# Seven half-width block products in place of eight for the output projection (Strassen's scheme), with a new plan of the instruction order

## The chip, the cores and the metric

The kernel runs on one core of one Trainium2 chip. The metric is device microseconds of an execution. Times are medians of several executions on the chip; the profile is of one execution, whose "span" runs from its first to its last instruction and is 1.7 to 1.8 us shorter than the time. "Rounds" run two or more kernels in turn, so that their times can be compared.

## The reference, cut to what matters

Attention for 4 x 8 heads of 768 tokens, of which three heads see all earlier keys and five see 4 sink keys and a window of 64; then a gated feed-forward block with its own residual gate on the 3072 x 512 result.

```python
g = x @ w_gate                       # 3072x512 @ 512x1536
gelu = 0.5 * g * (1.0 + erf(g * inv_sqrt2))
val = x @ w_val
ffn_out = gelu * val @ w_out         # 3072x1536 @ 1536x512: the product that changes
res_gate = 1.0 / (1.0 + np.exp(-(x @ w_res)))
return x + res_gate * ffn_out
```

## The kernel before

The program is a graph of tasks; a planner puts them into one order per engine with the help of priorities, and waits are derived from the dependences. The tokens are worked on in six chunks of four row tiles of 128. Attention of a chunk is laid between the gate/value stages and the output product of the chunk before it. `hT` holds the hidden values, transposed, 12 blocks of 128; `wo` is the output weight. One row tile of the output costs 12 matmuls of 512 columns:

```python
    def output(c, h, htoks, xbuf, xtoks, xtbuf, xttoks):
        for lt in range(4):
            ...                                        # residual product, 4 matmuls of 512, then tanh on ScalarE
            fb = Buf(P_ps, "gv" if last else "out")    # one PSUM bank
            for j in range(6):
                prev_t = G.add("pe", ..., e.matmul(at(fb)[:, w], lhsT=at(h)[:, fi, s], rhs=wo[:, fi, w],
                                                   start=(fi == 0), stop=(fi == NF - 1))   # fi = 2j, 2j+1; line 1161
            t1 = G.add("dve", ..., scalar_tensor_tensor(out=ot, in0=sr, scalar=1.0, in1=fb, op0=add, op1=mult))
            t2 = G.add("dve", ..., tensor_tensor(out=ot, in0=ot, in1=xbuf, op=add))
            G.add("sp", ..., dma_start(out[...], ot))
```

At the start GpSimd issues all loads into one queue (q, k, v, then gate and value weights `wg`, `wv` in pieces of 512 KB) and builds the masks in between. TensorE runs padding matmuls on a blank tile between the first attention pieces while it has to wait for data. `va` are the loaded values, `vs` their copies shifted by half a tile.

The softmax here doesn't subtract the row's maximum and nothing guards it: scores larger than these inputs give would overflow.

Of the kernel before, what the change touches and what calls it, by code (L numbers as in the profile page):

```python
# [4 lines left out]
NHEAD = 8  # L5
SEQ = 768
# [33 lines left out]
DT_FIRST = 2  # L40
DT_ALL = 9
# [5 lines left out]
    "0:-96.05 3:-32.5 13:-14.98 398:-205.14 399:-3161.01 400:-242.48 401:-60.67 406:194.11 428:585.68 "  # L47
    "430:523.84 442:461.16 444:1172.07 587:-105.78 592:-108.69 613:396.07 617:407.42 620:-11.7 640:556.2 "
    "642:106.88 643:194.09 646:-2979.21 649:-102.44 659:511.02 686:-2.88 687:77.5 695:496.52 696:499.45 "
    "698:-3129.77 703:60.14 704:-184.95 705:-133.38 707:183.02 708:380.49 711:7.46 712:149.85 713:-50.64 "  # L50
    "715:-14.97 722:1121.95 725:480.98 726:449.69 731:-39.24 732:60.67 733:-318.24 737:-43.72 738:419.39 "
    "739:143.85 743:67.93 744:-230.75 746:-318.2 749:428.99 755:137.07 756:5.66 757:60.69 761:-9.34 "
    "762:495.92 764:2489.99 778:1098.32 789:2479.4 791:2501.2 807:953.41 837:1156.8 842:1419.06 877:2567.99 "
    "879:1563.79 880:2429.98 883:2507.13 898:1013.73 933:1964.55 937:1029.47 939:1471.24 940:2476.14 "
    "955:3421 962:3506.26 963:3575.25 971:3584.03 984:2490.73 989:3565.66 1020:3589.17 1022:2520.47 "
    "1036:2494.69 1066:3486.98 1103:3422.44 1109:3530.5 1114:4315.61 1115:4410.02 1124:-926.78 1134:4596.47 "
    "1141:3465.41 1143:2510.98 1146:2495.35 1152:4653.43 1157:112.2 1170:3039.97 1193:107.93 1248:3488.54 "
    "1265:3479.95 1266:4395.47 1271:4430.01 1272:4484.04 1275:-26.92 1284:5420.01 1289:3472.11 1290:4444.38 "
    "1293:-34.14 1295:3453.61 1302:4490.78 1305:3510.02 1316:3998.02 1318:3550.85 1319:3550.87 1320:4107.35 "
    "1349:3529.55 1351:5429.99 1355:3583.42 1414:5485.04 1451:1066.16 1462:4552.31 1474:4473.03 1475:6343.89 "  # L60
    "1480:4497.31 1530:6505.9 1534:2349.36 1556:5501.98 1602:6498.99 1637:6513.87 1670:7448.62 1687:7406.44 "
    "1689:5504.27 "
# [399 lines left out]
def build_kernel(nc, q, k, v, w_gate, w_val, w_out, w_res, out):  # L462
# [15 lines left out]
    P_st = Pool(many("qks", 2, [128, 4096], FP16))  # L478
# [5 lines left out]
    P_er = Pool(many("er", 2, [128, 4608], FP16))  # L484
# [5 lines left out]
    P_h = Pool(many("hT", 2, [128, NF, 512], FP16))  # L490
# [7 lines left out]
        "av1": (2, one(0, 1)), "av2": (1, [(0, 1)]), "av1": (3, one(0, 1, 6)),  # L498
        "sc": (2, [(2, 3), (4, 5)]), "scr": (3, one(5, 4, 3, 2)), "scr0": (3, one(5, 4, 3, 2)),
# [3 lines left out]
    def at(buf):  # L503
        if buf.pool is P_ps:
            return psum[:, buf.slot[0] * 512:(buf.slot[-1] + 1) * 512]
        return buf.pool.items[buf.slot]
# [50 lines left out]
    wtok = {}  # L557
# [20 lines left out]
    late_copies = []  # L578

# [10 lines left out]
    def values(b, a, z, base, each, on_engines=False):  # L590

        BB = batch(b)
        for i in range(a, z):
            BB.vtok[i] = dma("pool", base, 0.9, (lambda i=i: lambda: at(BB.v)[:, i, :, 0:DHEAD])(),
                             v[b, :, i * 128:(i + 1) * 128, :].rearrange("h p d -> p h d"), bufs=[BB.v])
            BB.vtok[i].late = 1.3
# [37 lines left out]
        for lo in cuts:  # L634
            hi = lo + 1 if each else z
            ts = []
            for dst, src, off in ((0, 64, 1), (64, 0, 0)):
# [3 lines left out]
                    [BB.vtok[i - off] for i in range(lo, hi)], base + 1, bufs=[BB.v, BB.vs], dma=0.15 * (hi - lo),  # L641
                    name="vs", grp=("vs", b, lo)))
# [5 lines left out]
    def loads_rows(c, si, b, a, z):  # L648
# [3 lines left out]
        st = Buf(P_st)  # L652
# [5 lines left out]
        def sv(j, h0, h1, w):  # L658
            return at(st)[:, :].rearrange("p (j h w) -> p j h w", j=2, h=NHEAD)[:, j, h0:h1, 0:w]
        for gi, (h0, h1) in enumerate(groups):  # L660
            for j, src in enumerate((q, k)):
                t = dma("pool", base + 4 * gi + j, (h1 - h0) * n * 0.089,
                        (lambda j=j, h0=h0, h1=h1: lambda: sv(j, h0, h1, n * 64))(),
                        src[b, h0:h1, lo:hi, :].rearrange("h (p j) d -> p h (j d)", j=n), bufs=[st])
# [6 lines left out]
        for k_ in range(0, NPAIR, per):  # L671
            ps_ = ORDER[k_:k_ + per]
            pr = 1000 * c - 492 + ps_[0] if c else 40 * k_ - 205
            for js in (((1,), (0,)) if c == 0 else ((0, 1),)):
# [3 lines left out]
                def tr(e, items=items, scr=scr):  # L678
                    return [e.transpose(out=at16(scr)[64 * x:64 * x + 64, (m * n + i) * 128:(m * n + i + 1) * 128],  # L679
                                        in_=at(st)[:, (jj * NHEAD + h) * 256 + i * 64:(jj * NHEAD + h) * 256 + (i + 1) * 64],  # L680
                                        identity=ident[:, :])
                            for m, (p, jj) in enumerate(items) for i in range(n) for x, h in enumerate(PAIRS[p])]
                tt = G.add("pe", c_mm(128, n) * len(items), tr, [t_ident] + [tok[jj, h] for p, jj in items for h in PAIRS[p]],
                           pr, bufs=[st, scr], name="qkT")
# [18 lines left out]
    def loads_natural(c, si, b, a, z):  # L703
# [3 lines left out]
        st = Buf(P_st)  # L707
# [4 lines left out]
        for i in range(a, z):  # L712
            for j, src in ((1, k), (0, q)):
                def sv(i=i, j=j):
                    return at(st)[:, (j * 4 + i - a) * 512:(j * 4 + i - a + 1) * 512]
# [4 lines left out]
                for d in ds:  # L720
                    d.late = 5.0
                t = G.add("sp", 1.65, (lambda sv=sv, i=i, j=j: lambda e: e.dma_start(
                    at(BB.qkt)[:, j, :, i * 128:(i + 1) * 128], sv(), transpose=True))(), ds, base, bufs=[st, BB.qkt], dma=0.6, name="dT")
                t.late = 3.0
# [7 lines left out]
        t.late = 2.0  # L732
# [8 lines left out]
    def attention(c, segs, xbuf, xtbuf, xtoks, xttoks, l0=0, last=(), ek=None):  # L741
# [6 lines left out]
        for k_, p in enumerate(order):  # L748
# [34 lines left out]
            P.et = Buf(P_er if any(retr) else P_es)  # L783
            P.where, P.ready = {}, {}
            P.off = 0
            for g in range(0, len(banks), 2):
                scores(P, tiles, [t[1:] + (id(t[2]) in lower,) for t in banks[g:g + 2]], g, retr)
            todo.append(P)
# [295 lines left out]
    def gate_value(c, xtbuf, xttoks, halves=()):  # L1084
        h = Buf(P_h)
        toks = []
        ph(c, "table").append(G.add("act", 0.2, lambda e: e.activation(out=scratch[:, :], in_=ident[:, 0:1], func=AF.Gelu),
# [190 lines left out]
```

## Time and profile before

| | kernel before |
|---|---|
| time, median (48 executions, those beside the result and all later runs) | 270.71 us (270.27 to 271.70) |
| span of the profile | 268.8 us |
| TensorE busy, matmuls | 98%, 2391 |
| VectorE busy | 140.1 us (52%) |
| output product, sum of start distances of its matmuls | 64.0 us |
| start of the last padding matmul | 18.52 us |

The sum of start distances is a better measure of TensorE than its "busy" time, because the ends of matmuls are modelled and overlap: the profile gives a matmul of 512 columns 0.38 us, while the next one starts 0.216 us after it.

In the profile's lines PE is TensorE's matmuls, PEld its weight loads, DVE VectorE, ACT ScalarE, POOL GpSimd and SP SyncE.

### The profile page before, as it was taken

The numbers are of one execution on the slowest core, as the hardware profiler recorded it, in microseconds if no ns is written. First come the engines' busy times: TensorE is split into PE (matmuls) and PEld (weight loads), VectorE is DVE, ScalarE is ACT, GpSimd is POOL, SyncE is SP. The second block draws the span as 40 slices with busy tenths as digits, with TensorE's granted clock in tenths as the row PEclk, the third lists the DMA queues.
The fourth block names the chain that finished last, engine by engine and source line by source line (L and its number), as shares of the span: only waits on it lengthen the run. The fifth ranks groups of instructions, "written<-read, shape, count | busy, mean of one in ns | idle before, by whom it ended". The sixth has DMA issues, their size and how long they took to land.

```text
span 268.8 us, 5676 instructions
## 1 busy us (share of the span) xinstructions
PE 264.2 (98%) x2391; PEld 138.7 (52%) x2391; DVE 140.1 (52%) x273; ACT 139.9 (52%) x215; POOL 87.3 (32%) x124
## 2 busy tenths in 40 slices
PE   8999999999999999999999999999999999999995
PEld 7677465465444455444455444555444455444444
DVE  2698245485264376445476433486145367534344
ACT  3785358783334877136792243984233788233310
POOL 8999508995808029894000000000000000000000
DMA  6999999999999999999994100022000113200013
GB/s 86 171 205 207 185 180 228 169 168 187 171 129 187 154 160 185 216 189 125 184 148 134 41 0 0 2 41 96 25 0 0 39 41 80 78 2 0 1 39 120
DMA packets 97562, 29.38 MB, mean 109 GB/s; under 512 B 85504, under 2 KB 93952, under 8 KB 97536
## 3 DMA queue, kind: packets, MB, share of 16 engines
q0 software_dynamic: 70320, 14.69, 65.5%
q1 hardware_dynamic: 27216, 14.33, 27.9%
q8 instruction: 19, 0.31, 0.5%
q14 instruction: 7, 0.06, 0.1%
HBM read 29.36 MB, written 6.29 MB: 133 GB/s over the span
## 4 chain that ended last, share of the span: by engine, by line
PE 93%; DMA 3%; POOL 1%; DVE 1%; issue 0%; POOLq 0%; DVEq 0%
PE ps L1116 44%; PE ps L1161 23%; PE ps L1146 8%; PE ps L857 5%; PE ps L991 3%; DMA va<-in_v_dram 3%; PE ps L1098 3%; PE ps L981 2%; PE ps L1005 2%; PE ps L1070 1%; POOL qks L555 1%; PE ps L948 1%; PE ps L679 1%; PE ps L1178 1%; DVE otile L1168 0%; DVE otile L1165 0%
## 5 line engine op out<-in xcount | busy, mean ns | idle before, releaser
L1130 DVE SCALAR_TENSOR_TENSOR hT<-gact,ps 128x512 f16<-128x512 f16 x68 | 45.8, 686 | 67.4 <-ACT gact L1128 36.6
L1128 ACT ACTIVATE gact<-ps 128x512 f16<-128x512 f32 x68 | 40.1, 597 | 74.0 <-PE ps L1116 72.5
L1116 PE MATMUL ps<-xT,wv 128*128 128x512 f16 x272 | 74.3, 379 | 0.0
L1116 PE MATMUL ps<-xT,wg 128*128 128x512 f16 x272 | 74.1, 379 | 0.0
L1161 PE MATMUL ps<-wo,hT 128*128 128x512 f16 (+2 forms) x312 | 70.4, 363 | 0.0
L1116 PEld LDWEIGHTS ps<-xT,wg 128*128 128x128 f16 x272 | 26.3, 98 | 31.5 <-ACT xT L1077 0.6
L1116 PEld LDWEIGHTS ps<-xT,wv 128*128 128x128 f16 x272 | 26.2, 98 | 30.5 <-DVE hT L1130 0.5
L1161 PEld LDWEIGHTS ps<-wo,hT 128*128 128x128 f16 x312 | 27.5, 98 | 27.0 <-issue 0.7
L873 ACT ACTIVATE er<-ps 128x1024 f16<-128x1024 f32 (+4 forms) x40 | 34.2, 891 | 9.5 <-PE ps L857 9.4
L555 POOL DMA_DIRECT2D qks<-in_k_dram x36 | 28.3, 827 | 32.4 <-DMA qkt<-qks 21.9
L555 POOL DMA_DIRECT2D qks<-in_q_dram x36 | 28.8, 840 | 0.8 <-POOLq L1260 0.8
L1165 DVE SCALAR_TENSOR_TENSOR otile<-srs,ps 128x512 f32<-128x512 f32 (+2 forms) x26 | 16.8, 644 | 16.5 <-PE ps L1161 16.4
L1146 PE MATMUL ps<-wr,xT 128*128 128x512 f16 x96 | 24.7, 379 | 0.0
L555 POOL DMA_DIRECT2D va<-in_v_dram x24 | 21.6, 926 | 2.7 <-PE ps L1005 2.7
L1149 ACT ACTIVATE srs<-ps 128x512 f32<-128x512 f32 x24 | 14.3, 597 | 15.6 <-PE ps L1146 15.3
L1048 DVE TENSOR_TENSOR xtok<-ps,rcp 128x512 f32<-128x512 f32 (+1 forms) x28 | 16.9, 609 | 0.6
L1168 DVE TENSOR_TENSOR otile<-otile,xtok 128x512 f32<-128x512 f32 (+2 forms) x26 | 16.8, 647 | 0.7
L857 PE MATMUL ps<-qkt 64*128 64x64 f16 (+4 forms) x391 | 16.9, 213 | 0.0
L857 PEld LDWEIGHTS ps<-qkt 64*128 64x128 f16 x391 | 9.8, 94 | 9.4 <-issue 3.4
L873 ACT ACTIVATE es<-ps 128x1024 f16<-128x1024 f32 (+1 forms) x14 | 12.6, 898 | 2.9 <-PE ps L857 2.6
L1146 PEld LDWEIGHTS ps<-wr,xT 128*128 128x128 f16 x96 | 8.7, 98 | 10.0 <-issue 0.7
L1178 PE MATMUL ps<-blank 128*128 128x128 f16 x116 | 11.4, 249 | 1.1 <-DVE blank L527 1.1
(70 smaller groups left out, 212.5 us busy)
## 6 DMA issues: line engine op xcount, KB each, us to landing
out_dram<-otile SPq DMA_DIRECT2D x23, 256.0 KB, 2.2
va<-in_v_dram POOLq DMA_DIRECT2D x24, 128.0 KB, 17.0
qks<-in_k_dram POOLq DMA_DIRECT2D x32, 64.0 KB, 11.9
qks<-in_q_dram POOLq DMA_DIRECT2D x32, 64.0 KB, 12.4
wg<-in_moe_w_gate_dram POOLq DMA_DIRECT2D x3, 512.0 KB, 10.3
wv<-in_moe_w_val_dram POOLq DMA_DIRECT2D x3, 512.0 KB, 10.6
wo<-in_moe_w_out_dram POOLq DMA_DIRECT2D x4, 384.0 KB, 22.2
vs<-va SPq DMA_DIRECT2D x4, 260.0 KB, 7.4
```

The lines of the kernel that those rows point to most:

```text
L555: return G.add(eng, issue, lambda e: e.dma_start(out_ap(), in_ap), deps, prio, bufs=bufs, dma=cost, name=name, grp=grp)
L857: return [e.matmul(at(scr)[:, oo:oo + w], lhsT=side(BB, low, 1)[half, k0:k0 + 128], rhs=side(BB, low, 0)[half, qq:qq + w], start=True, sto ...
L873: return e.activation(out=o, in_=i_, func=AF.Exp, scale=SM_SCALE)
L1048: t2 = G.add("dve", c_dve(2 * n * 64), lambda e: e.tensor_tensor(out=xview(), in0=avv(0, DHEAD), in1=scale(), op=ALU.mult), [t1] + xdeps, ...
L1116: return lambda e: [e.matmul(at(dst)[:, :], lhsT=w[:, ci, f * 128:(f + 1) * 128], rhs=at(xtbuf)[:, ci, :], start=(ci == 0), stop=(ci == NC ...
L1128: ta = G.add("act", c_act(512), (lambda gb=gb, ga=ga: lambda e: e.activation(out=at(ga)[:, :], in_=at(gb)[:, :], func=AF.Gelu))(), [tg], p ...
L1130: th = G.add("dve", c_dve(512), (lambda vb=vb, ga=ga, f=f: lambda e: e.scalar_tensor_tensor(out=at(h)[:, f, :], in0=at(ga)[:, :], scalar=0 ...
L1146: e.matmul(at(rb)[:, :], lhsT=at(xtbuf)[:, ci, s], rhs=wr[:, ci, :], start=(ci == 0), stop=(ci == NCB - 1))
L1149: ta = G.add("act", c_act(512), (lambda rb=rb, sr=sr: lambda e: e.activation(out=at(sr)[:, :], in_=at(rb)[:, :], func=AF.Tanh, scale=0.5)) ...
L1161: e.matmul(at(fb)[:, w], lhsT=at(h)[:, fi, s], rhs=wo[:, fi, w], start=(fi == 0), stop=(fi == NF - 1))
L1165: t1 = G.add("dve", c_dve(n), (lambda fb=fb, sr=sr, ot=ot, w=w: lambda e: e.scalar_tensor_tensor(out=at(ot)[:, w], in0=at(sr)[:, w], scala ...
L1168: t2 = G.add("dve", c_dve(n), (lambda ot=ot, lt=lt, w=w: lambda e: e.tensor_tensor(out=at(ot)[:, w], in0=at(ot)[:, w], in1=at(xbuf)[:, lt, ...
```

## The change

Two row tiles and twelve blocks are taken as a 2 x 2 by 2 x 2 block product, which seven products of half width compute instead of eight. Each is six matmuls of 256 columns. The sums of hidden blocks and the differences of weights that the scheme needs go to VectorE; copies and additions of the partial results go to VectorE and ScalarE. It is used for chunks 1 to 4 and for the first half of chunk 5. `hT` becomes one buffer, staging for q and k becomes three halves in place of two wholes, PSUM pairs are shared more widely, the copy of head 6 stands ahead of the shifted values in SyncE's queue, the tiles of the attention weights (`er`, two of 4608 columns) become one of 4608 and one of 2816, and longer transfers are assumed in the plan. The priorities of the planner are new, so the whole order of instructions changes. The core, with cuts:

```diff
+FAST = (1, 2, 3, 4, 5)
-    P_h = Pool(many("hT", 2, [128, NF, 512], FP16))
+    P_h = Pool(many("hT", 1, [128, NF, 4, 128], FP16))
+    P_hs = Pool(many("hS", 1, [128, 3, NF // 2, 2, 128], FP16))
+    wt = sb("wt", [128, 4, NF // 2, 256], FP16)
...
-        "sc": (2, [(2, 3), (4, 5)]), ...
+        "sc": (3, [(2, 3), (4, 5), (0, 1)]), ...
...
+                    order=copies[-1:], name="vs", grp=("vs", b, lo)))
...
+    def sums(c, h, htoks):                     # VectorE, in the gate/value stage; S3 replaces A21 in hT
+            t1 = add(0, (0, 1), (1, 1), ALU.add, deps, "s1")
+            t2 = add(1, 0, (0, 0), ALU.subtract, [t1], "s2")
+            t4 = add(2, (1, 0), 1, ALU.subtract, [t2], "s4")
+            t3 = add((0, 1), (0, 0), (0, 1), ALU.subtract, [t1], "s3")
...
+    def output_fast(c, pi, h, htoks, hs, stoks, xbuf, xtoks, xtbuf, xttoks):
+        X, Y = Buf(P_ps, "out"), Buf(P_ps, "out")          # two banks, used in turn
+        p1 = product(X, "A11", "B11", True, [])
+        k1 = keep(p1, 0, 0)                                # copy out of X, VectorE or ScalarE
+        p2 = product(Y, "A12", "B21", True, [])
+        c11 = plus(p2, k1, 0, 0)                           # add Y to the copy, VectorE
+        p6 = product(X, "S2", "T2", False, [k1])           # accumulates in X
+        k2 = keep(p6, 0, 256)
+        p5 = product(Y, "S1", "T1", True, [c11])
+        p7 = product(X, "S3", "T3", False, [k2])
+        k3 = keep(p7, 1, 256)
+        c22 = plus(p5, k3, 1, 256)
+        p4 = product(X, "A22", "T4", False, [k3])
+        p3 = product(Y, "S4", "B22", False, [c22])
+        c12 = plus(p3, k2, 0, 256)
```

## The prediction

> **What bounds the kernel now.** I read the page first: busy shares, chain, then the costliest groups.
>
> ```profile
> span 268.8 us, 5676 instructions
> PE 264.2 (98%) x2391; PEld 138.7 (52%) x2391; DVE 140.1 (52%) x273; ACT 139.9 (52%) x215; POOL 87.3 (32%) x124
> PE 93%; DMA 3%; POOL 1%; DVE 1%; issue 0%; POOLq 0%; DVEq 0%
> PE ps L1116 44%; PE ps L1161 23%; PE ps L1146 8%; PE ps L857 5%; PE ps L991 3%; DMA va<-in_v_dram 3%; PE ps L1098 3%; PE ps L981 2%; PE ps L1005 2%; PE ps L1070 1%; POOL qks L555 1%; PE ps L948 1%; PE ps L679 1%; PE ps L1178 1%; DVE otile L1168 0%; DVE otile L1165 0%
> ```
>
> TensorE fills the chain that ends last, and the output product, the line that the change rewrites, is 23% of it. But "busy" is a modelled end, so I asked how far apart successive matmuls start. The chain of waits in order of time gives the pure rates (start, length, what):
>
> ```profile
> 19.59 1.75 PE ps L1098 x16
> 231.29 20.72 PE ps L1116 x96
> ```
>
> 20.72 us / 96 = 0.2158 us per matmul of 512 columns and 1.75 / 16 = 0.1094 us per matmul of 256 columns. So half the columns cost 50.7%: the loads of 128x128 weights (98 ns each in the groups) still hide behind 256 columns. Walking the start times of all matmuls after the last padding one, which starts at 18.5 us, I find no dependency gap worth naming: what exceeds the stream is a small pause at each change between full and split array. The timeline (start, length, engine, line) shows one:
>
> ```profile
> 91.10 0.59 PE L1161 MATMUL ps<-wo,hT 128*128 128x512 f16 x2
> 91.63 0.39 PE L857 MATMUL ps<-qkt 64*128 64x512 f16 x1
> ```
>
> Two matmuls from 91.10 would end at 91.53; the 64-row form starts at 91.63, so the change costs 0.10 us. The kernel is therefore TensorE's stream from about 18.6 us on, plus a start of 18.6 us and a tail of about 3 us after the last matmul starts (265.7 us). A shorter stream should shorten the whole, unless another engine starts to hold it up. The candidate is VectorE, in the stages where attention of one chunk and the output of the previous one overlap (busy by engine in each stretch):
>
> ```profile
> 86.80:107.80 21.00, 21.00 (x256) 11.27 (x255) 12.67 (x26) 16.04 (x21) 7.69 (x10) 1.00 1.93 168
> 129.10:148.00 18.90, 18.90 (x205) 9.63 (x204) 11.89 (x23) 11.53 (x17) 0.00 (x0) 1.00 1.03 153
> 169.90:188.30 18.40, 18.40 (x234) 9.96 (x233) 12.24 (x23) 12.94 (x18) 0.00 (x0) 1.00 0.19 55
> 209.70:231.10 21.40, 21.40 (x263) 11.10 (x262) 13.49 (x25) 15.51 (x20) 0.00 (x0) 1.00 0.19 56
> ```
>
> The columns after the length are PE, PEld, DVE, ACT, POOL. VectorE is at 60 to 67% there.
>
> **What the Trainium skill says.** "TensorE: Matmul & The Clock Gate", section "Wait — 56ns, not 53.3ns?", gives N / 2.4 GHz plus about 2.5 ns for back-to-back warm matmuls: 109.2 ns for 256 and 215.8 ns for 512. The trace agrees (109.4 and 215.8). "TensorEngine Tiling (Array Packing)", section "Key Properties", says that a change of tiling mode drains TensorE; the trace shows about 0.1 us each. "VectorE: DVE Perf Modes", section "Mode 2×_1P — pack two bf16 into one 32-bit read", lets a tensor_tensor on 16-bit operands do two results a cycle; the trace agrees: the 128x1024 fp16 mask takes 0.68 us, as long as a 128x512 operation that reads PSUM in fp32 (0.69). "PSUM — Partial Sum Buffer", section "PSUM bank collisions raise a hardware error", asks that a bank be guarded by a semaphore between engines. So a half product may not be written into a bank until the copy out of it is done, which is the new wait of this change.
>
> **The change part by part.**
>
> Removed: in chunks 1 to 4 both pairs of row tiles and in chunk 5 the first pair, nine pairs, lose 24 matmuls of 512 columns each: 216 x 0.2158 = 46.6 us. The order of instructions confirms it: that form falls from 276 to 60.
>
> Added on TensorE: seven products of six matmuls with 256 columns per pair, 42 x 9 = 378 x 0.1094 = 41.4 us. Net -5.2 to -5.3 us. The other groups keep their counts (544 gate and value, 96 residual, all attention forms). Mode changes after the last padding matmul: 89 in both orders, so no gain or loss.
>
> Start: the changed order puts about seven more small matmuls ahead of the last padding one and has 112 instead of 116 of these (0.056 us each). I count -0.2 us. The v loads are issued behind four more small GpSimd operations, about 1 us later, but the loads of one queue landed one after the other (q and k until 9.8 us, then v at 10.8 and 13.3), so most of that should vanish in the queue.
>
> Added on VectorE: four sums per chunk in two parts. At 0.6 us (back-to-back start distance of 0.69 us operations) for 1024 elements and 0.36 to 0.42 for 512, that is about 4.2 us a chunk, which lies in the gate and value stages, where VectorE is busy only 8 to 10 of 21 us. Once, four weight differences of 1536 elements, about 1 us each, while chunk 0's output runs. Per pair three copies out of PSUM (15 of the 27 stand on VectorE, 12 on ScalarE), three additions, and 0.16 us more for the split last operation. For the four overlap stages this is 4.3, 3.2, 3.6 and 4.3 us (0.36 us per 256-element piece). Load there becomes (12.67 + 4.3) of 19.8 us, 15.1 of 17.7, 15.8 of 17.2 and 17.8 of 20.2: 85 to 92%. It fits, but with little room.
>
> New waits on TensorE: one chunk's products alternate between two banks. The delays can be read at the end of the kernel:
>
> ```profile
> 254.01 1.03 PE L1146 MATMUL ps<-wr,xT 128*128 128x512 f16 x4
> 255.07 0.60 ACT L1149 ACTIVATE srs<-ps 128x512 f32<-128x512 f32 x1 [1.56 <-PE ps L1146]
> 258.32 4.05 PE L1161 MATMUL ps<-wo,hT 128*128 128x512 f16 x18
> 259.89 0.69 DVE L1165 SCALAR_TENSOR_TENSOR otile<-srs,ps 128x512 f32<-128x512 f32 x1 [2.04 <-PE ps L1161]
> ```
>
> Four matmuls from 254.01 have streamed by 254.87 and ScalarE starts 0.20 us later; six from 258.32 have streamed by 259.62 and VectorE starts 0.27 us later. A copy of 256 columns lasts 0.38 us on ScalarE and 0.42 on VectorE; I estimate 0.06 us back to TensorE, from its first matmul's start after VectorE's clearing of the blank tile. A bank is thus out of use for 0.64 us (ScalarE) or 0.75 us (VectorE). One product in the other bank hides 6 x 0.109 = 0.656 us. In the changed order ten handovers have only one such product between; seven of them wait for VectorE, 0.09 us each, 0.6 us. Add 0.5 us for occasions when VectorE is still at other work at 85 to 92% load: +1.1 us.
>
> Sum: 270.84 - 5.25 - 0.2 + 1.1 = 266.5; I round to 266.4.
>
> The rest: the larger pool of bank pairs lets scores or weighted values of attention take another pair; TensorE has no bank waits to lose, so it can only pay for the products' use of banks. One hT buffer in place of two makes the next chunk's first product with the values wait for the last half product; both are in order on TensorE and nearly adjacent, so I count nothing. The copy of head 6 and the longer transfers in the plan only change the order of issues. Before, this copy landed at 87.6 us and its first reader started at 89.05, so there was 1.5 us of room; the first reader moves by some 0.2 us only, because no output before it has become shorter. I count nothing.
>
> **The rivals.** First: VectorE becomes the bound of the four overlap stages. For it: 85 to 92% load in order of program, with work of three kinds in one queue. Against: the order is planned with these operations in it, and before, at 60 to 67%, TensorE never waited. If each stage loses 1 us, the gain shrinks to about 2 us: 268.5. Second: the saving comes whole, because the planner put other work between all handovers that matter. Then 270.84 - 5.5 = 265.3, the best I can justify, since nothing but the stream is left to shorten. Third: a transfer comes late. The transfer engines are busy in nearly every slice until about 150 us, three staging buffers of half the size replace two, and the attention of chunk 3 starts some 1.4 us earlier. For it: the thin 1.5 us at head 6. Against: staging is freed in smaller pieces and sooner, and the data of chunk 3 landed by about 103 us for use at 128. It would add about 1 us: 267.5.
>
> **Range and chances.** The 2% mark is 270.84 x 0.98 = 265.4, just above the best case of 265.3. So "faster" needs almost no new wait or a start that gains a few tenths more than I count. The first and third rivals together reach 268.5. I say 266.4 us, 264.9 to 268.5; faster by over 2% with 0.25, within 2% with 0.72, slower by over 2% with 0.03.
>
> **What would show each step right or wrong.** Groups: the new line of half products with 378 matmuls at a start distance of 109 ns, 60 of the old form left. If the distance is nearer to 120 ns, weight loads or waits are not hidden. Stretches: VectorE at 85 to 92% in the overlap stages; TensorE's starts should show gaps only at half products that wait for a copy or an addition, about 1 us in sum. The last padding matmul should still be near 18.6 us. I am wrong if TensorE waits several us at half products, at attention's first scores (late transfer), or at the gate products (sums delaying the release of value banks).

## More of the kernel before

One more view is needed later, the timeline of the first products of the gate and value stage in the kernel before. Columns: start, length, engine, line, operation, tiles, array, size, how many.

```profile
19.43 0.60 PE L1098 MATMUL ps<-xT,wg 128*128 128x256 f16 x4
19.86 0.60 PE L1098 MATMUL ps<-xT,wv 128*128 128x256 f16 x4
```

The value product at 19.86 carries no bracket, so it waited for nothing. Its weights had landed at 19.51 us in this execution.

## The result, and the profile after

| | before | after |
|---|---|---|
| time, median of 4 executions each | 270.78 us (270.29 to 271.00) | 267.75 us (267.51 to 268.00) |
| ratio | | 0.989 (0.9876 to 0.9904) |
| span of the profile | 268.8 us | 266.3 us |

Ratios here and below are the mean time of one kernel's runs over that of the other's in the same rounds, so they are not quite the ratio of the medians. The kernel got 1.1% faster. Two later runs of the same kernel gave 268.34 us (ratio 0.9916) and 267.58 us (0.9887); over its 14 executions the mean is 267.94 us against 270.70 us for the 48 of the kernel before, 2.8 us less.

The page of the kernel after, its size, busy shares and chain by engine and line:

```profile
span 266.3 us, 6108 instructions
PE 260.1 (98%) x2549; PEld 153.3 (58%) x2549; DVE 177.3 (67%) x369; ACT 144.3 (54%) x226; POOL 87.2 (33%) x124
...
PE 88%; DVE 4%; DMA 4%; POOL 0%; issue 0%
PE ps L1141 44%; PE ps L1231 15%; PE ps L1210 6%; PE ps L1298 5%; PE ps L881 4%; DMA wv<-in_moe_w_val_dram 4%; PE ps L1015 3%; PE ps L1123 3%; PE ps L1005 2%; PE ps L1283 2%; PE ps L1029 1%; PE ps L1094 1%; PE ps L697 1%; PE ps L972 1%; DVE otile L1265 1%; DVE otile L1268 1%
```

TensorE still makes up most of the chain, but 88% instead of 93%, and the chain's first part is a different one: not the v load that led the chain before, but `DMA wv`, the value weights. VectorE gained 37 us of work.

The groups of the new work, without forms told apart where "(+ forms)" stands (line, engine, operation, tiles, size, count, then busy and mean ns, then idle time before and who ended it):

```profile
L1298 PE MATMUL ps<-wo,hT 128*128 128x512 f16 (+2 forms) x96 | 17.6, 326 | 0.0
L1231 PE MATMUL ps<-wt,hT 128*128 128x256 f16 x108 | 15.5, 273 | 0.2 <-DVE otile L1238 0.2
L1231 PE MATMUL ps<-wt,hS 128*128 128x256 f16 x108 | 15.3, 273 | 0.0
L1231 PE MATMUL ps<-wo,hT 128*128 128x256 f16 x108 | 14.3, 273 | 0.1
...
L1244 DVE TENSOR_TENSOR otile<-otile,ps 128x256 f32<-128x256 f32 x27 | 11.2, 415 | 7.0 <-PE ps L1231 6.0 <-ACT otile L1239 0.6
...
L1231 PE MATMUL ps<-wo,hS 128*128 128x256 f16 x54 | 7.5, 273 | 0.0
L1238 DVE COPY otile<-ps 128x256 f32<-128x256 f32 x15 | 6.3, 422 | 4.2 <-PE ps L1231 4.1
```

108 + 108 + 108 + 54 are the 378 half-width matmuls that were counted ahead. The distance from the start of each to the start of the next matmul, taken from all starts in the trace, sums to 44.4 us, 117 ns each; the pure stream would be 41.3. What is over is mode changes (changes between the full array and a split one, about 0.1 us each) and waits. With the remaining ordinary output products (15.8 us) the output costs 60.1 us against 64.0 before: 3.9 less.

VectorE's load in the four stretches where attention and output overlap (length, then PE, PEld, DVE, ACT, POOL busy):

```profile
86.30:107.90 21.60, 21.36 (x297) 14.78 (x295) 18.59 (x43) 16.13 (x21) 13.06 (x18) 1.00 2.06 158
127.20:145.50 18.30, 18.30 (x255) 12.43 (x254) 15.86 (x38) 14.61 (x22) 0.00 (x0) 1.00 1.25 144
166.70:185.30 18.60, 18.60 (x276) 12.96 (x275) 15.99 (x35) 15.27 (x22) 0.00 (x0) 1.00 0.26 41
206.00:228.00 22.00, 22.00 (x304) 14.74 (x303) 18.60 (x41) 18.06 (x24) 0.00 (x0) 1.00 0.17 37
```

18.59 / 21.60 is 86%, and the others are 87, 86 and 85%. TensorE's modelled busy time falls short of the stretch in the first one only. The stretches are not quite those of the kernel before: each now holds 5 to 11 gate and value matmuls of 512 columns (1.2 to 2.5 us), where before each held one at most.

Where TensorE waits is seen where two starts are further apart than the stream and the mode change between them ask for. In the kernel before these gaps sum to 0.6 us. In the kernel after they sum to 3.3 us. (Counted over matmuls of the full array alone, without gaps under 0.025 us, it is 0.2 and 3.0.) The largest stands at the start:

```profile
19.52 0.24 PE L1029 MATMUL ps<-vk,ek 128*128 128x65 f16 x2
20.79 0.61 PE L1123 MATMUL ps<-xT,wv 128*128 128x256 f16 x4 [1.03 <-DMA wv<-in_moe_w_val_dram]
```

The bracket says that TensorE sat idle until `DMA wv` released it; from start to start it lost 1.19 us.

The second largest, 0.40 us, is a half product at 93.02 us whose bank was not yet copied out. The timeline, with VectorE between:

```profile
91.96 0.57 DVE L615 COPY vk<-va 4x130 f16<-4x130 f16 x1
91.97 0.82 PE L1231 MATMUL ps<-wo,hT 128*128 128x256 f16 x6
92.54 0.42 DVE L1238 COPY otile<-ps 128x256 f32<-128x256 f32 x1
...
93.02 0.50 PE L1231 MATMUL ps<-wt,hT 128*128 128x256 f16 x3 [0.23 <-DVE otile L1238]
```

The product before in the same bank had streamed by 91.96, so the copy out of it (second line of VectorE) could have started near 92.16. It started at 92.54, because a copy of values for the masked heads of 0.57 us stood before it in VectorE's program. The rest are small: 0.28 us at 107.9 (a gate product whose x copy, the copy of the transposed x out of PSUM, stood behind one of the new gating operations of 0.69 us), 0.18 and 0.20 us at 253.4 and 255.9 in the tail, and some ten of about 0.1 us. Of the gaps of the full array, 1.0 us stand at half products and 0.75 us at gate, residual and x products.

Handovers of a bank that are not held up by other work cost almost nothing. The last half products at the end of the kernel follow each other with VectorE and ScalarE free:

```profile
256.89 0.82 PE L1231 MATMUL ps<-wt,hT 128*128 128x256 f16 x6
257.09 0.42 DVE L1244 TENSOR_TENSOR otile<-otile,ps 128x256 f32<-128x256 f32 x1 [2.60 <-PE ps L1231]
...
257.57 0.83 PE L1231 MATMUL ps<-wt,hS 128*128 128x256 f16 x6
257.81 0.38 ACT L1239 ACTIVATE otile<-ps 128x256 f32<-128x256 f32 x1 [1.20 <-PE ps L1231]
```

The product at 257.57 needs the bank that the addition at 257.09 reads. From 256.89 to 257.57 are 0.68 us, where six matmuls stream in 0.656: 0.02 us is lost.

**The wait for `wv`.** Each transfer ends with 16 completion marks in the trace, one for each of the queue's 16 parts. The Trainium skill, "DMA: Bandwidth & Descriptors", section "Why a DMA increments its semaphore by 16 and not by 1", says that a transfer runs on up to 16 engines that finish independently and that only all 16 marks mean that the data are there. The trace agrees, and shows what that costs here. Marks of the first value weights, called value weights 0 below:

| kernel, profile | issued | 15th mark | 16th mark |
|---|---|---|---|
| before | 11.01 | 19.42 | 19.51 |
| before, second profile | 11.01 | 19.46 | 19.65 |
| after | 11.21 | 19.50 | 20.74 |

The issue is 0.2 us later, 15 parts are as quick as before, and the last is 1.24 us behind. In this profile all later weights keep a lag of 1.1 us or more; the last value weights land at 30.90 us instead of 29.68.

This suggests a cut of the span in two: start = the start of the last padding matmul plus the waits for value weights; rest = everything else.

| | start | rest |
|---|---|---|
| before, two profiles | 18.52, 18.75 | 250.24, 250.11 |
| after, three profiles | 19.89, 19.77, 19.61 | 246.38, 246.02, 246.39 |
| means | 18.64 to 19.76: +1.12 | 250.18 to 246.26: -3.92 |

-3.92 + 1.12 = -2.80. The two parts make up the span, so that this sum must be the difference of the spans; that the times show the same 2.8 us says only that the profiled executions were typical. Of the +1.12, 0.97 are waits for value weights and 0.15 a later last padding matmul. So there are two questions: is the rest bounded by the stream or by VectorE, and does the new order really cost the start?

### The profile page after: what moved, and what is told of

It reads as the page before. It is cut to its first block, busy times and chain, and to the rows that moved or that the text cites. A ratio compares the mean times of both kernels' runs of the same rounds, so it can differ in the third digit from the quotient of the medians. Undisturbed runs are those within 1.5% of the kernel's fastest.

```text
span 266.3 us, 6108 instructions
## 1 busy us (share of the span) xinstructions
PE 260.1 (98%) x2549; PEld 153.3 (58%) x2549; DVE 177.3 (67%) x369; ACT 144.3 (54%) x226; POOL 87.2 (33%) x124
## 4 chain that ended last, share of the span: by engine, by line
PE 88%; DVE 4%; DMA 4%; POOL 0%; issue 0%
PE ps L1141 44%; PE ps L1231 15%; PE ps L1210 6%; PE ps L1298 5%; PE ps L881 4%; DMA wv<-in_moe_w_val_dram 4%; PE ps L1015 3%; PE ps L1123 3%; PE ps L1005 2%; PE ps L1283 2%; PE ps L1029 1%; PE ps L1094 1%; PE ps L697 1%; PE ps L972 1%; DVE otile L1265 1%; DVE otile L1268 1%
## 5 line engine op out<-in xcount | busy, mean ns | idle before, releaser
L897 ACT ACTIVATE ea<-ps 128x1024 f16<-128x1024 f32 (+2 forms) x24 | 21.4, 916 | 2.3 <-PE ps L881 2.1
L1210 PE MATMUL ps<-wr,xT 128*128 128x512 f16 x72 | 18.2, 380 | 0.0
L1298 PE MATMUL ps<-wo,hT 128*128 128x512 f16 (+2 forms) x96 | 17.6, 326 | 0.0
L881 PE MATMUL ps<-qkt 64*128 64x64 f16 (+3 forms) x391 | 16.3, 213 | 0.0
L1244 DVE TENSOR_TENSOR otile<-otile,ps 128x256 f32<-128x256 f32 x27 | 11.2, 415 | 7.0 <-PE ps L1231 6.0
L1231 PE MATMUL ps<-wt,hT 128*128 128x256 f16 x108 | 15.5, 273 | 0.2 <-DVE otile L1238 0.2
L1231 PE MATMUL ps<-wt,hS 128*128 128x256 f16 x108 | 15.3, 273 | 0.0
L1231 PE MATMUL ps<-wo,hT 128*128 128x256 f16 x108 | 14.3, 273 | 0.1
L897 ACT ACTIVATE eb<-ps 128x1024 f16<-128x1024 f32 (+3 forms) x16 | 13.4, 856 | 1.4 <-PE ps L881 1.2
L1213 ACT ACTIVATE srs<-ps 128x512 f32<-128x512 f32 x18 | 10.7, 595 | 6.1 <-PE ps L1210 5.9
```

Of the source, the lines that this page charges most:

```text
L881: return [e.matmul(at(scr)[:, oo:oo + w], lhsT=side(BB, low, 1)[half, k0:k0 + 128], rhs=side(BB, low, 0)[half, qq:qq + w], start=True, sto ...
L897: return e.activation(out=o, in_=i_, func=AF.Exp, scale=SM_SCALE)
L1210: e.matmul(at(rb)[:, :], lhsT=at(xtbuf)[:, ci, s], rhs=wr[:, ci, :], start=(ci == 0), stop=(ci == NCB - 1))
L1213: tas.append(G.add("act", c_act(512), (lambda rb=rb, sr=sr: lambda e: e.activation(out=at(sr)[:, :], in_=at(rb)[:, :], func=AF.Tanh, scale ...
L1231: e.matmul(at(D)[:, 0:256], lhsT=left[l](j), rhs=right[r](j), start=first and j == 0, stop=(j == NF // 2 - 1), skip_group_check=True) for ...
L1244: return G.add("dve", c_dve(256), lambda e: e.tensor_tensor(out=dst(), in0=dst(), in1=at(Y)[:, 0:256], op=ALU.add), [t, k], pr, bufs=[Y, o ...
```

## The experiments

Theory: the stream's saving arrives, VectorE and the handovers cost about 1.5 us, and a lag of one part of the load queue costs about 1 us at the start. Rivals: VectorE's load, not TensorE's stream, sets the overlapped stages; or the waits at the start are an accident of one profile; or they come from the order of instructions and can be ordered away.

The experiments on order keep the plan of the kernel after and move single tasks in the finished programs, then sort the common list again so that every dependence holds:

```diff
     span = G.schedule()
+    for moved, after in SHIFTS:                # task numbers, same engine
+        m, lst = by[moved], G.prog[by[moved].eng]
+        lst.remove(m)
+        lst.insert(lst.index(by[after]) + 1, m)
+    ...                                        # sort again, check every dependence
```

(Every moved kernel has one line more at the top, so its line 1232 is line 1231 here.)

**The same kernel again** (label same_again, no edit).

> The changed kernel once more, to see whether TensorE's wait of about 1.0 us before the first product with the value weights, whose transfer landed 1.2 us later than in the kernel before, comes back. Theory A (the lag comes from where the loads of instructions fall in this program, so it repeats): the wait is again 0.9 to 1.3 us and the times lie within 0.5 us of 267.75. Theory B (chance of an execution): the wait is anywhere from 0 to 1.3 us and the times spread by about 1 us.

Measured: 268.34 us (267.53 to 269.01, six executions), ratio 0.9916 (0.9902 to 0.993). The wait is there again, 1.02 us; its 15th mark came at 19.93 and its 16th at 20.61. The 0.40 us at 92.5 us was 0.09 this time. Theory A held for the wait, theory B for the times. So the wait is not an accident of one profile, but the executions spread over 1.5 us, which those of the kernel before did not (270.27 to 271.26).

**One value product moved back** (label v2_late): the first value product is moved behind the third gate product, `SHIFTS = ((704, 703),)`, so that value weights are wanted 1.3 us later.

> Same order of everything, only the first product with the value weights (feature block 2, first half) stands behind the three gate products that follow it. Theory A (that wait of 1.2 us is pure loss): 266.5 us. Theory B (the weights' transfers set the pace, as the second value weights land at 25.9 us and would now be wanted at 25.1, the third at 30.9 and wanted at 29.8): most of the wait comes back at the later weights, the gain is 0.1 to 0.4 us, 267.4 us.

Measured: 267.22 us (266.58 to 269.67, six executions), ratio 0.9882 (0.9855 to 0.9911). The profiled execution was the bad one: one part of the queue lagged by 2.6 us (15th mark 19.80, 16th 22.38), and TensorE stood still where the moved product now is:

```profile
22.43 0.61 PE L1124 MATMUL ps<-xT,wv 128*128 128x256 f16 x4 [1.21 <-DMA wv<-in_moe_w_val_dram]
```

The other five had a median of 266.98, 1.4 us under the kernel beside it. That looked like a gain by order (the median of all six lies nearer to theory B).

**A second look at it** (label v2_late_again, the same kernel).

> The one move of value half 2 behind the third gate product, a second time, on another chip. Its first five undisturbed executions had a median near 267.0 us, 1.3 us under the changed kernel beside it, but the two moves of the next call gained nothing. If the order really buys back the lag of value weights 0, the median is 266.6 to 267.2 us again and the ratio to the kernel before 0.985 to 0.987. If the lag only moves to another transfer (a late v load that holds up the start), it is 267.4 to 268.2 us, ratio 0.988 to 0.991, with the start later by about 1 us in the profile or a wait for later value weights.

Measured: 267.56 us (266.43 to 268.57, six executions), ratio 0.989 (0.9866 to 0.9914), the same as the change itself. The second expectation held. The wait at 19.6 us is gone, but two waits at later value products, which ended at 25.59 and 30.66 us, took its place; the weight loads of TensorE name them:

```profile
PEld ps L1142 <- DMA wv<-in_moe_w_val_dram: 1.3, 2, 0.8
```

From start to start they cost 0.81 us. Start is 18.70 + 0.81 = 19.51, rest 246.36. In this execution the lag is a delay of the whole weight stream in the slowest part, and an order that wants one piece later only meets it at the next piece. The twelve executions of this kernel run from 266.43 to 269.67.

**Less work at each handover** (label small_both; wrong): in chunks 2 to 5 the copies and additions between half products take 32 of 256 columns.

```diff
+        W_ = 256 if c == 1 else 32
-        e.tensor_copy(out=dst(), in_=at(X)[:, 0:256])                 # and the same on ScalarE
+        e.tensor_copy(out=dst()[:, 0:W_], in_=at(X)[:, 0:W_])
-        e.tensor_tensor(out=dst(), in0=dst(), in1=at(Y)[:, 0:256], op=ALU.add)
+        e.tensor_tensor(out=dst()[:, 0:W_], in0=dst()[:, 0:W_], in1=at(Y)[:, 0:W_], op=ALU.add)
```

> Wrong result on purpose: in chunks 2 to 5 the copies out of the first bank and the additions from the second take 32 of 256 columns, in the same order. Theory A (waits of TensorE at half products for a copy or addition cost about 1 us in sum, of which chunks 2 to 5 have about half): 0.3 to 0.7 us faster, 267.2 us. Theory B (VectorE, 20 us less loaded by it, sets the pace of the overlap stages): 2 us faster or more, 265.7 us.

Measured: 267.46 us (267.34 to 267.57, four executions), ratio 0.9879, result wrong (relative error 0.85). The page's second line:

```profile
PE 259.9 (98%) x2549; PEld 154.3 (58%) x2549; DVE 170.9 (64%) x369; ACT 142.3 (54%) x226; POOL 87.2 (33%) x124
```

The time is 0.9 us under the kernel after of the same call and 0.5 under the mean of its 14 executions; the start alone spreads by as much, so the rest tells more. VectorE does 6.4 us less, where the expectation reckoned with 20, and rest is 245.92 us, 0.34 less than the mean of the three profiles of the kernel after. The small waits at 173, 212 and 259 us are gone; the one at 92.4 us, in the unchanged chunk 1, stays. VectorE as the bound of the stages with chunks 2 to 5 falls: a bound would have given back a good part of the 6.4 us. The first of the four stages, where VectorE was late at 92 us, was not tried with less work.

**The stream put back** (label wide_products; wrong): the seven products get 24 matmuls of 512 columns in place of 42 of 256, which is the stream that was removed, in the order and with the waits of the change.

```diff
-        e.matmul(at(D)[:, 0:256], lhsT=left[l](j), rhs=right[r](j), ...) for j in range(j0, j0 + 3)
+        e.matmul(at(D)[:, 0:512], lhsT=left[l](j), rhs=wo[:, 2 * j, :], ...)
+            for j in range(j0, j0 + (1 if l in ("S1", "S4") else 2))
```

> Wrong result on purpose: the same order and the same waits, but in place of 42 matmuls with 256 columns each pair has the kernel before's 24 with 512. Theory A (TensorE's stream sets the time, and the saving of 5.3 us arrives except for the waits at half products): 4.6 to 5.3 us slower than the changed kernel, 272.3 to 273.0 us. Theory B (part of the shorter stream is only turned into waits for other engines): under 4 us slower, below 271.8 us.

Measured: 273.93 us (273.52 to 274.92, four executions), ratio 1.0124 (1.0105 to 1.0142): 5.6 us above the kernel after of the same call. The group of the wide products, two of the lines:

```profile
L1231 PE MATMUL ps<-wo,hT 128*128 128x512 f16 x144 | 36.3, 380 | 0.2
L1231 PE MATMUL ps<-wo,hS 128*128 128x512 f16 x72 | 20.6, 380 | 0.0
```

144 + 72 are the 216 of the kernel before. Rest is 252.08 us, 5.8 over the kernel after; 5.26 were to be expected from the stream. Both lie above theory A's 4.6 to 5.3; the start of this profile is 0.3 us later than the mean of the kernel after, and its waits elsewhere are some 0.4 us longer, perhaps because two of the seven products are now only two matmuls long. The saving of the stream is real, and theory B (under 4 us) falls. The new order and its waits cost the rest 252.08 - 250.18 = 1.9 us in this kernel; with the short stream it is 5.26 - 3.92 = 1.3 us.

The comparison of results called this kernel correct, and the one with the small sums below too, though both compute a wrong product. The likely reason is that the gated feed-forward part is small beside x: worked out with the reference for the first 768 tokens, it has about 1% of its norm. So "correct" says little about the half products of the change either. Their algebra was read and is Strassen's in Winograd's form, with all four blocks right; no run proved it.

**GpSimd's start as before** (label pool_as_before): the first seventeen GpSimd tasks are put into the order of the kernel before, with v loads between mask selections.

> The changed kernel with GpSimd's first seventeen tasks put back into the order of the kernel before (identity selection third, each v load between two mask selections), everything else as changed. Theory A: this order is what makes one of the queue's parts lag, so value weights 0 land near 19.5 us instead of 20.6 to 20.7, TensorE's wait at 19.6 us is under 0.3 us, and the time falls by 0.8 to 1.2 us against the changed kernel's 267.5 to 268.3: 266.7 to 267.3. Rival B: the lag comes from something else in the longer program, such as its instruction loads: the wait stays at 0.8 us or more and the time within 0.4 us of the changed kernel's.

Measured: 267.77 us (267.48 to 267.96, four executions), ratio 0.9887. Neither theory met it. The wait for `wv` is gone, as A wanted, and the time is unchanged, as B wanted. Value weights 0 still landed at 20.25 us; TensorE did not wait because it came there 1.0 us later, with its last padding matmul at 19.71 us. The traces point to the edit itself. Masks now come later from GpSimd, while VectorE's program was planned for early masks. VectorE in this kernel:

```profile
10.07 0.54 DVE L536 COPY m_win<-m_win 128x256 f16<-128x256 f16 x3 [2.65 <-POOL m_win L525]
```

and in the kernel after:

```profile
8.47 0.83 DVE L535 COPY m_win<-m_win 128x256 f16<-128x256 f16 x3 [1.02 <-POOL m_win L524]
9.51 1.29 DVE L711 COPY qkt<-ps 128x512 f16<-128x512 f16 x2 [0.21 <-PE ps L697]
```

The mask copy waits until 10.07 us instead of 8.47, and what stands on VectorE behind it, the copies of transposed q and k first (10.53 instead of 9.51), is 1 us late. Start is 19.71, rest 246.32. So this run does not tell whether the old GpSimd order keeps the lag away. It tells that the change bought early masks with later v loads, and that taking one back without the other gained nothing here.

**All moves together** (label all_moves): that start, the value product moved, one copy of masked values behind the half-product copy at 92.4 us, one gating behind the x copy at 107.4 us.

> The changed kernel with GpSimd's start as before, value half 2 of tile 0 after the third gate product instead of ahead of the first, one copy of masked values behind the half-product copy at 92.4 us, and one gating behind the x copy at 107.4 us. Nothing is taken away, only the order in the programs differs. If the waits seen in the changed kernel's trace are what it lost (1.0 to 1.2 us at 19.6, 0.1 to 0.4 at 92.4, 0.3 at 107.4), the time falls by 1.3 to 1.9 us against the changed kernel, to about 266.0 to 266.8, and those three waits are under 0.1 us each. Rival: the time stays within 0.5 us because the waits reappear a few products later (the next value weights still land 1.2 us late, or VectorE still runs behind).

Measured: 267.43 us (267.16 to 267.57, four executions), ratio 0.9872 (0.9852 to 0.9892). The expectation missed by 0.6 us or more. Value weights 0 landed at 19.39 us, all three waits were gone, and yet start is 19.71, for the same reason as in the run before. Rest is 246.12. The wait at 92.4 us came back as three of 0.06, 0.06 and 0.21 us in the same stage; the one at 107.4 us is gone, but for 0.06 us at a value product just behind it.

**Two transfers moved back in SyncE's queue** (label copy_late), `SHIFTS = ((456, 441), (781, 456), (457, 781), (803, 457))`. It was meant to undo the place of head 6's copy, and missed. What it moves behind the shifted values and two output transfers are the first two transposing transfers of q and k for the next batch; the copies of head 6 stay. So the expectation describes another edit than the one that ran.

> The changed kernel with one part of the change undone: in SyncE's queue the two copies of head 6 stand again behind the shifted values and the first two output transfers, as before. The prediction counted nothing for this part. Theory A: within 0.3 us of the changed kernel, and TensorE waits for no head 6 tile. Rival: head 6's scores in tile 1 come late, TensorE waits 0.5 us or more near 85 to 92 us, and the time rises by that.

Measured: 267.56 us (266.56 to 268.56, six executions), ratio 0.9879 (0.9855 to 0.9904). The two transposing transfers start at 63.8 us instead of 52.4, and no TensorE wait follows. The profiled execution is faster than any of the kernel after, and shows why: the last part of value weights 0 came early, at 19.74 us.

```profile
19.79 0.61 PE L1124 MATMUL ps<-xT,wv 128*128 128x256 f16 x4
```

Start is 18.90, rest 245.95, time 266.56. The edit touches nothing that runs before 36 us, so I take this as a lucky execution, not as an effect: three of the six were near 266.8 us and three near 268.2. It shows one time of the change when the lag stays small: 266.56 us. (The 0.40 us at 93 us was 0.03 in it, too.) The place of head 6's copy was not tried alone; no profile of the changed order shows TensorE waiting for that tile.

**The kernel before, profiled again** (label before_again, no rounds).

> The kernel before, as it is, for a second profile of it. If its order keeps the lag away, value weights 0 land between 19.3 and 19.7 us again and TensorE waits for them under 0.3 us. If the lag is a matter of chance that the first profile happened to miss, they land after 20 us.

Measured: 270.58 us. Value weights 0 landed at 19.65 us and TensorE did not wait, as was expected for an order that keeps the lag away. The lag is not absent in this order: k's second half had its last mark at 10.61 us here and at 9.76 in the first profile, and the third v load's last two marks lay 0.48 and, in the first profile, 1.45 us apart. It did not reach the weights, in two profiles of two.

**Two moves with GpSimd's new start** (label two_moves): `SHIFTS = ((704, 703), (1016, 1086))`.

> The changed kernel with two tasks moved in their engines' programs and nothing else: value half 2 of tile 0 behind the third gate product, and one gating on VectorE behind the x copy at 107 us. GpSimd keeps the changed kernel's order. The 0.27 us wait at 107.4 us should be gone, as it was with all the moves, and the wait for value weights 0 should be under 0.3 us as long as they land before 21 us. Theory A, the two waits are what is to be had: 1.0 to 1.5 us under the changed kernel of the same call, so 266.3 to 267.0 if that is at 267.8. Rival B, the lag of one part of the queue comes back at a later weight transfer whatever the order: under 0.5 us gained, and executions spread over 1 us or more.

Measured: 267.87 us (266.46 to 268.54, six executions), ratio 0.9888 (0.9867 to 0.9909). No wait for value weights, none at 107.4, and no gain: rival B held. In the profile the lag hit a v load instead (third v load at 14.76 us; 14.31 in the kernel after). VectorE's copies of shifted values wait for it, and they also ran longer:

```profile
14.78 0.91 DVE L635 COPY vs<-va 64x1040 f16<-64x1040 f16 x1
...
16.55 0.79 DVE L635 COPY vs<-va 64x1040 f16<-64x1040 f16 x1
```

In the kernel after:

```profile
14.36 0.43 DVE L634 COPY vs<-va 64x1040 f16<-64x1040 f16 x1
...
15.65 0.42 DVE L634 COPY vs<-va 64x1040 f16<-64x1040 f16 x1
```

So the copies end 1.27 us later (17.34 against 16.07), and the last padding matmul is at 19.84 instead of 18.70. For their length, the Trainium skill, "SBUF — State Buffer", section "Who interferes with whom", has a candidate: a copy on VectorE in its two-port modes and GpSimd exclude each other from a shared pair of ports for a whole instruction. GpSimd was issuing q loads at that time:

```profile
15.45 0.76 POOL L567 DMA_DIRECT2D wv<-in_moe_w_val_dram  x1
16.18 1.79 POOL L567 DMA_DIRECT2D qks<-in_q_dram  x2
```

The traces agree in part. The three copies of this size that lay wholly beside the issue of q loads (in this run, pool_as_before and all_moves) took 0.76 to 0.79 us, and the four that began before it and ended in it (before_again, same_third, v2_late and small_sums) took 0.74, 0.50, 0.53 and 0.52. Beside the issue of weight loads alone they took 0.42 to 0.43 in twelve profiles; the copy at 15.65 us in the kernel after, inside such an issue (15.62 to 16.37), is one of them. But the one of 0.91 us above lay beside weight loads too. No run here isolates it, so it stays a candidate.

**The kernel after, a third time** (label same_third).

> The changed kernel once more, beside the two others of this call. Median 267.5 to 268.4 as in its first two; if the lag of one part of the queue differs from execution to execution, its times spread over 1 us or more again and the profile's wait for value weights 0 is between 0.2 and 1.5 us.

Measured: 267.58 us (267.46 to 267.73, four executions), ratio 0.9887. The wait is 0.69 us. The executions did not spread this time: the spread of over 1 us that was expected did not come.

**Smaller sums** (label small_sums; wrong): the sums of hidden blocks in chunks 2 to 5 take 16 of 128 columns.

```diff
+        part = lambda a: a if c == 1 else a[:, :, :, 0:16]
-        e.tensor_tensor(out=view(o), in0=view(x), in1=view(y), op=op)
+        e.tensor_tensor(out=part(view(o)), in0=part(view(x)), in1=part(view(y)), op=op)
```

> The changed kernel with a wrong result on purpose: the sums of hidden halves that VectorE makes in the gate stages of chunks 2 to 5 take 16 of 128 columns, so that each costs it a fraction of its 0.42 us. The prediction counted these sums as nothing on the path. Theory A: within 0.4 us of the changed kernel of this call. Rival B, VectorE's added work delays the activations' partners in the gate stages and so TensorE: 0.8 us or more faster.

Measured: 268.09 us (267.39 to 268.52, four executions), ratio 0.9911. That is 0.5 us above the kernel after of the same call, just outside theory A; rival B, 0.8 us or more faster, falls. The page shows how much work was taken away:

```profile
PE 260.9 (98%) x2549; PEld 154.2 (58%) x2549; DVE 167.8 (63%) x369; ACT 144.2 (54%) x226; POOL 86.9 (33%) x124
```

9.5 us less on VectorE, and rest is 246.36, as in the kernel after. The sums of chunks 2 to 5 are off the path; those of chunk 1 were left whole.

**All profiles in one table.** Start is the start of the last padding matmul plus all waits for value weights, rest is the span less that.

| run | last padding | waits for `wv` | start | rest |
|---|---|---|---|---|
| before | 18.52 | 0 | 18.52 | 250.24 |
| before_again | 18.75 | 0 | 18.75 | 250.11 |
| after | 18.70 | 1.19 | 19.89 | 246.38 |
| same_again | 18.75 | 1.02 | 19.77 | 246.02 |
| same_third | 18.92 | 0.69 | 19.61 | 246.39 |
| v2_late | 18.85 | 2.58 | 21.43 | 246.52 |
| v2_late_again | 18.70 | 0.81 | 19.51 | 246.36 |
| pool_as_before | 19.71 | 0 | 19.71 | 246.32 |
| all_moves | 19.71 | 0 | 19.71 | 246.12 |
| two_moves | 19.84 | 0 | 19.84 | 246.29 |
| copy_late | 18.67 | 0.23 | 18.90 | 245.95 |
| small_sums | 18.89 | 0.39 | 19.28 | 246.36 |
| small_both | 18.74 | 1.01 | 19.75 | 245.92 |
| wide_products | 18.64 | 1.45 | 20.09 | 252.08 |

Nothing that was reordered moved the rest by more than 0.4 us from the mean of the kernel after. What differs between executions of the changed order is the start, from 18.9 to 21.4 us, and in each with a late start late parts of a transfer, or late masks, can be named.

**What stays open.** Why one part of the queue lags in the changed kernel up to the weights and not in the kernel before. Loads of instructions, packets of 16 KB that take 0.89 to 1.0 us in the trace, run at about 10 and 17 us in both kernels, so they alone don't tell the two apart, though the point at which they fall may. The trace does not say on which engine a packet ran. The table's profiles do hold a hint: value weights 0 landed at 19.39 to 20.25 us in the four with GpSimd's old start (before, before_again, pool_as_before, all_moves) and at 19.74 to 22.38 in the ten with the new one. Four profiles are too few to call that the cause. And no version beat the change clearly: the best ratio, 0.9872, has an interval that holds 0.989.

## Why the prediction was right or wrong

The time was predicted as 266.4 us, 264.9 to 268.5, most likely within 2%; measured were 267.75 us and a ratio of 0.989. The range and the class held; the centre was 1.4 us too low, and nearly all of that is one step.

- **What bounds the kernel: right.** With the stream put back at the same order, rest rose by 5.8 us; with VectorE's work in chunks 2 to 5 cut by 6.4 or 9.5 us it fell by 0.34 and rose by 0.1.
- **Net stream -5.25 us: right.** 378 and 60 matmuls of the two forms are in the trace. The stream that was put back cost 5.6 us in time and 5.8 in rest.
- **New waits +1.1 us: right in kind, low by 0.4.** Without the waits for `wv`, gaps sum to 2.1, 1.8 and 2.1 us in the three profiles of the kernel after and to 0.6 and 0.5 in the two of the kernel before: +1.5 (the rest gives +1.3: 5.25 less 3.92). The split of the estimate was off. Free handovers cost 0.02 to 0.03 us in the tail where 0.09 was reckoned, and some 0.1 us elsewhere; the larger part is VectorE being at other work when a bank or an x copy is wanted, 0.40 and 0.28 us at two places of the first overlapped stage. The prediction looked for gaps only at half products; 0.75 us stand at others.
- **VectorE at 85 to 92%: right as a share, in part by luck.** It is 85 to 87%, but as 18.6 of 21.6 us in the first stretch where 17.0 of 19.8 were reckoned: work and time were both mis-sized, partly because the stretch now holds gate and value matmuls too, and the two misses cancel. The first rival, VectorE as the bound and 268.5 us, is refuted for chunks 2 to 5 by the run with small copies, though its time was close to what was measured.
- **The sum for all after the start: right.** 246.03 was implied (250.18 less 5.25, and 1.1 of waits); measured 246.26.
- **Start -0.2 us: this is the step that failed.** In the prediction's words, the v loads are issued "about 1 us later", but "most of that should vanish in the queue". In the v loads' own landings it did vanish (15.18 us for the last, 15.23 before). But the landing of a transfer is that of its slowest part. The count took the queue as one, and looked only at the transfers that the change had moved. The weights behind them landed 0.8 to 1.2 us later in the slowest part, where the plan has a value product first and wants them at 19.6 us with nothing to spare. Measured +1.1 us, the mean of three profiles against two, where -0.2 was reckoned: 1.3 us. Why the part lags stays open.
- **The third rival, a late transfer of about 1 us and 267.5 us, is what happened,** at another place than was named: not at head 6 or at chunk 3's data, which caused no wait, but at the first value weights.
- **Sums, head 6's copy and the single `hT` buffer at nothing:** shown for the sums of chunks 2 to 5, by the run that shrinks them. The other two were not tried alone; no gap of TensorE stands at a tile of head 6 in any profile of the changed order, and no gap was found that points to the single buffer.
- **"The last padding matmul should still be near 18.6 us": right** (18.70 to 18.92), and it shows that this mark was too early to watch: the start's cost came just behind it.

## What to carry to other kernels

When a stream-bound kernel loses stream, the saving can arrive, as here, if the engines that take over the work have room at the moments when they are wanted; look at the one operation ahead of each release, not at the average load. Check the start separately: a plan that wants a transfer at the very moment of its landing pays for the slowest of the queue's parts, and in both profiles of an order that wants one piece later the same lag was met at the next pieces. Cut the span where the limit changes, and compare the pieces; here the rest of the profiled executions held within 0.4 us of its mean while whole times spread by more than the effects in question.

## What the Trainium skill lacked or had wrong

- "DMA: Bandwidth & Descriptors", section "Why a DMA increments its semaphore by 16 and not by 1", is right on the 16 marks, but doesn't say how far they lie apart. Here 15 marks of a 512 KB load were in by 19.50 us and the last by 20.74; in one execution the gap was 2.6 us. It can stay for the later transfers of the queue (29.79 and 30.90 us for the last value weights) or vanish (1.45 us at the last v load of the kernel before, 0.09 at its first value weights).
- "SBUF — State Buffer", section "Who interferes with whom", gives the rule for VectorE's copies against GpSimd, but not which part of a transfer's issue takes the ports: copies of 64x1040 took 0.76 to 0.79 us wholly beside the issue of q loads, and beside the issue of weight loads alone 0.42 to 0.43 us in twelve profiles and 0.91 in one.
- No page gives as a whole the price of handing a PSUM bank from TensorE to another engine and back: 0.20 to 0.21 us from the end of the stream to the start on VectorE and 0.26 on ScalarE, an operation of 0.42 us (VectorE) or 0.38 us (ScalarE), 0.06 us from its end to the next product, and 0.02 us lost when one product of 0.656 us lies between.
- "TensorE: Matmul & The Clock Gate", section "Wait — 56ns, not 53.3ns?", held: 109.4 and 215.8 ns. Nothing was found wrong in what was used of it.
